# Layer scale on one Trainium2 core: the first four rows of y loaded as two partition halves on two DMA queues

## Chip, cores and metric

The kernel runs on one core of a Trainium2 chip. The time is device time in microseconds (us) of one execution, as a median of several; the profile is of one further execution, taken by the hardware profiler. A core has engines that run their own instruction streams: TensorE (PE, matrix products), VectorE (DVE, elementwise work), ScalarE (ACT), GpSimd (POOL) and SyncE (SP). Transfers between HBM and the on-chip memory (SBUF, 128 partitions) are issued by SP and ACT, each on a DMA queue (ring) of its own, and are carried out by 16 DMA engines that both queues share.

## The reference

```python
B, S, D = 1024, 16, 512
x, y:  normal * 0.05, shape (B, S, D), bfloat16
gamma: 1e-4 * normal * 0.05, shape (D,), bfloat16

def reference(x, y, gamma):
    return x + gamma * y
```

x, y and the output have 16,384 rows of 512 bfloat16 values, 16.78 MB each.

## The kernel before

The 16,384 rows are spread over 128 partitions, so that each partition has 128 rows. They are cut into blocks of 4, 64 and 60 rows per partition (`BLOCKS`, line 7); within a block, a partition's rows are contiguous in HBM, so a transfer of rows 4 to 68 moves one run of 64 KB for every partition, and a transfer of rows 0 to 4 one run of 4 KB. All of y stays in SBUF, in `y_sb`. x goes into the smaller `x_sb`, parts of which are used twice.

The order of everything is written out by hand. `SP` (line 12) and `ACT` (line 20) list what the two queues carry, in order: `('y', a, b)` loads rows a to b of y, `('x', a, b, at)` loads rows a to b of x to row `at` of `x_sb`, `('g',)` loads gamma's one row of 1 KB, `('s', a, b)` stores rows a to b of the result. Below, y(0,4) stands for the load of rows 0 to 4 of y, and so on. SP carries y(0,4), y(4,68), x(4,68), y(68,128), x(68,120), x(120,128). ACT carries x(0,4), gamma, and the stores of 4 to 68, 0 to 4 and 68 to 128.

`ring` (line 113) issues such a list. The first `EARLY` entries of a list are moved to the front of the program, ahead of the engines' opening synchronisation (line 197 on): two on SP, one on ACT. Ahead of entry number `AHEAD` (the same 2 and 1) the engine waits for its `s_held` semaphore. TensorE gives it out: it waits for the landing of `HOLD`, y(0,4) (line 147), and then frees SP, ACT and VectorE (line 148). So x(4,68) on SP and gamma on ACT are issued only after y(0,4) has landed, and a load into a part of `x_sb` that was used before waits for the adds that read it (`frees`, line 102): x(68,120) waits for the add of rows 24 to 68, x(120,128) also for the add of rows 0 to 8. The stores wait for `s_go`, which TensorE gives when `RELEASE`, x(68,120), has landed (line 157), and for the adds of their rows.

TensorE multiplies a row of ones with gamma (line 152), which puts gamma on all partitions of a PSUM tile, and VectorE copies that to `gamma_sb` (line 154). VectorE then works through `DVE` (line 28) on pieces of 8, 16, 44, 52 and 8 rows: `m` multiplies a piece of y by gamma in place (line 180), `a` adds x (line 189). The order is the multiplies of pieces 0, 1, 2, then the adds of pieces 2, 0, 1, then the multiplies of 3 and 4 and the adds of 3 and 4. Piece 0, rows 0 to 8, needs both y(0,4) and y(4,68). The last store, of rows 68 to 128, needs the adds of pieces 3 and 4.

A wait is `_take`, line 35: wait until the semaphore has a value, and take that off again.

Of the kernel before, what the change touches and what calls it, by code (L numbers as in the profile page):

```python
# [8 lines left out]
PIECES = [8, 16, 44, 52, 8]  # L9


SP = [
    ('y', 0, 4),
    ('y', 4, 68),
    ('x', 4, 68, 4),
    ('y', 68, 128),
    ('x', 68, 120, 24),
    ('x', 120, 128, 0),
]
ACT = [('x', 0, 4, 0), ('g',), ('s', 4, 68), ('s', 0, 4), ('s', 68, 128)]  # L20

EARLY = (2, 1)

HOLD, AHEAD = ('y', 0, 4), (2, 1)

RELEASE = ('x', 68, 120, 24)

# [4 lines left out]
def _take(sem, n, eng):  # L32


    return eng.wait_ge(sem, n).then_inc(sem, -n)  # L35


def kernel(
    tc: tile.TileContext,
    x: bass.AP,  # L40
    y: bass.AP,
    gamma: bass.AP,
    out: bass.AP,
):

    nc = tc.nc
    P = nc.NUM_PARTITIONS
    tc.close()  # L50
    tc.compile()  # L51

    xf = x.flatten_outer_dims()
    yf = y.flatten_outer_dims()
    of = out.flatten_outer_dims()
    N, D = xf.shape
    rows = N // P
    n = len(PIECES)
    assert sum(PIECES) == rows
    starts = [sum(PIECES[:c]) for c in range(n + 1)]  # L60
    dt = xf.dtype
    edges = [sum(BLOCKS[:c]) for c in range(len(BLOCKS) + 1)]
    assert edges[-1] == rows

    def rows_of(t, a, b):

        c = max(c for c in range(len(BLOCKS)) if edges[c] <= a)
        assert b <= edges[c + 1]
        block = t[P * edges[c] : P * edges[c + 1]].rearrange("(p n) d -> p n d", p=P)
        return block[:, a - edges[c] : b - edges[c], :]  # L70

    gamma_row = nc.alloc_sbuf_tensor("gamma_row", [1, D], dt).ap()
    ones_row = nc.alloc_sbuf_tensor("ones_row", [1, P], dt).ap()
    gamma_sb = nc.alloc_sbuf_tensor("gamma_sb", [P, D], dt).ap()
    y_sb = nc.alloc_sbuf_tensor("y_sb", [P, rows, D], dt).ap()
    x_loads = [w for w in ACT + SP if w[0] == "x"]
    y_loads = [w for w in SP + ACT if w[0] == "y"]
    stores = [w for w in SP + ACT if w[0] == "s"]
    for loads in (x_loads, y_loads, stores):
        assert sum(w[2] - w[1] for w in loads) == rows  # L80
    x_rows = max(w[3] + w[2] - w[1] for w in x_loads)
    x_sb = nc.alloc_sbuf_tensor("x_sb", [P, x_rows, D], dt).ap()
    gamma_ps = nc.alloc_psum_tensor("gamma_ps", [P, D], mybir.dt.float32).ap()

    sem = nc.alloc_semaphore
    s_gamma, s_ones, s_ps, s_dve = sem("s_gamma"), sem("s_ones"), sem("s_ps"), sem("s_dve")
    s_load = {w: sem("s_" + "_".join(map(str, w[:2]))) for w in x_loads + y_loads}
    s_held = {nc.sync: sem("s_held_sp"), nc.scalar: sem("s_held_act"), nc.vector: sem("s_held_dve")}
    s_add, s_go, s_rel, s_end, s_out = sem("s_add"), sem("s_go"), sem("s_rel"), sem("s_end"), sem("s_out")
    added = [a for kind, *a in DVE if kind == "a"]  # L90
    order = {a[0]: k for k, a in enumerate(added)}

    def meets(a, b, c, d):
        return a < d and c < b

    def pieces_of(a, b):
        return [c for c in range(n) if meets(starts[c], starts[c + 1], a, b)]

    def x_at(row):
        return next(w[3] + row - w[1] for w in x_loads if w[1] <= row < w[2])  # L100

    def frees(w):

        c = set()
        for v in x_loads[: x_loads.index(w)]:
            lo, hi = max(v[3], w[3]), min(v[3] + v[2] - v[1], w[3] + w[2] - w[1])
            if lo < hi:
                c |= set(pieces_of(v[1] + lo - v[3], v[1] + hi - v[3]))
        return sorted(c)

    early = []

    def ring(eng, what, n_early, n_ahead):

        known, went = 0, False
        for k, w in enumerate(what):
            kind = w[0]
            if k == n_ahead:
                _take(s_held[eng], 1, eng)
            need = frees(w) if kind == "x" else pieces_of(w[1], w[2]) + list(w[3:]) if kind == "s" else []  # L120
            need = max((order[c] + 1 for c in need), default=0)
            if kind == "s" and not went:
                _take(s_go, 1, eng)
                went = True
            if need > known:
                eng.wait_ge(s_add, need)
                known = need
            if kind == "g":
                i = eng.dma_start(out=gamma_row, in_=gamma.unsqueeze(0)).then_inc(s_gamma, 16)
            elif kind == "x":  # L130
                to = x_sb[:, w[3] : w[3] + w[2] - w[1], :]
                i = eng.dma_start(out=to, in_=rows_of(xf, w[1], w[2])).then_inc(s_load[w], 16)
            elif kind == "y":
                r = slice(w[1], w[2])
                i = eng.dma_start(out=y_sb[:, r, :], in_=rows_of(yf, w[1], w[2])).then_inc(s_load[w], 16)
            else:
                r = slice(w[1], w[2])
                i = eng.dma_start(out=rows_of(of, w[1], w[2]), in_=y_sb[:, r, :]).then_inc(s_out, 16)
            if k < n_early:
                early.append(i.ins)  # L140

    ring(nc.sync, SP, EARLY[0], AHEAD[0])
    ring(nc.scalar, ACT, EARLY[1], AHEAD[1])


    nc.vector.memset(ones_row, 1.0).then_inc(s_ones, 1)  # L146
    _take(s_load[HOLD], 16, nc.tensor)
    for s_one in s_held.values():
        nc.tensor.sem_inc(s_one, 1)
    _take(s_ones, 1, nc.tensor)  # L150
    _take(s_gamma, 16, nc.tensor)
    nc.tensor.matmul(gamma_ps, ones_row, gamma_row, start=True, stop=True).then_inc(s_ps, 1)  # L152
    _take(s_ps, 1, nc.vector)
    nc.vector.tensor_copy(out=gamma_sb, in_=gamma_ps).then_inc(s_dve, 1)  # L154
    _take(s_dve, 1, nc.vector)

    _take(s_load[RELEASE], 16, nc.tensor)
    nc.tensor.sem_inc(s_go, 1)
    nc.tensor.sem_inc(s_rel, 1)

    landed, open_mults = set(), 0

    def need(loads, c):
        for w in loads:
            if w not in landed and meets(starts[c], starts[c + 1], w[1], w[2]):
                if w == RELEASE:
                    _take(s_rel, 1, nc.vector)
                elif w == HOLD:
                    _take(s_held[nc.vector], 1, nc.vector)
                else:  # L170
                    _take(s_load[w], 16, nc.vector)
                landed.add(w)

    for kind, *args in DVE:
        c = args[0]
        yt = y_sb[:, starts[c] : starts[c + 1], :]
        if kind == "m":
            need(y_loads, c)
            g = gamma_sb[:, None, :].to_broadcast([P, PIECES[c], D])
            nc.vector.tensor_tensor(out=yt, in0=yt, in1=g, op=MULT).then_inc(s_dve, 1)  # L180
            open_mults += 1
        else:
            need(x_loads, c)
            if open_mults:
                _take(s_dve, open_mults, nc.vector)
                open_mults = 0
            at = x_at(starts[c])
            xt = x_sb[:, at : at + PIECES[c], :]
            nc.vector.tensor_tensor(out=yt, in0=xt, in1=yt, op=ADD).then_inc(s_add, 1)  # L189


    nc.scalar.sem_inc(s_end, 1)
    _take(s_end, 1, nc.sync)
    _take(s_add, n, nc.sync)
    _take(s_out, 16 * len(stores), nc.sync)

    main = nc.main_func.blocks[0].instructions
    names = {i.name for i in early}
    for b in nc.main_func.blocks[1:]:
        for i in [i for i in b.instructions if i.name in names]:  # L200
            b.instructions.remove(i)
    for k, i in enumerate(early):
        main.insert(1 + k, i)
# [30 lines left out]
```

## Time and profile before

| | |
|---|---|
| median of 3 runs | 119.87 us (119.71 to 120.06) |
| the profiled execution | 119.55 us |
| its span, first to last instruction | 118.2 us |
| multiplies, line 180 | 5 instructions, 34.7 us |
| adds, line 189 | 5 instructions, 34.7 us |
| DMA packets | 1442, 50.33 MB |
| landing after issue: y(0,4), 512 KB | 3.4 us |
| landing after issue: x(0,4), 512 KB | 4.2 us |
| landing after issue: last store, rows 68 to 128 | 23.8 us |

The span is cut into 40 slices in the page; the two rows below give the busy share of VectorE and of the 16 DMA engines in each (tenths).

```profile
DVE  0000200089999969999999999999999900000000
...
DMA  6999889988899879879969696898899889799793
```

A packet is counted whole in the slice in which it starts, so the DMA row swings. Lines of the profile that begin with an engine's name and a q (SPq, ACTq, DVEq) are that engine's sequencer: it issues transfers and waits. "Landing" is the arrival of the last of a transfer's completions.

### The profile page before, as it was taken

Reading aid. Unit: us, or ns where it says so; the run is one execution under the profiler, and the core shown is the slowest. Engines: PE = TensorE matmul, PEld = TensorE weight load, DVE = VectorE, ACT = ScalarE, POOL = GpSimd, SP = SyncE. Lnnn points to the kernel's source line nnn. Section 1 sums busy time; section 2 is a strip of 40 time slices with the busy share of each in tenths; the row PEclk is TensorE's granted clock in tenths of the full one; section 3 lists DMA queues with packets and bytes.
Section 4 is the critical chain, followed back from the end, with each engine's and each line's share of the span. In section 5 each row is a group of like instructions: output and inputs, shape, how many; then the busy total and the mean of one; then the engine's idle time right before and its main releaser. Section 6 shows DMA issues by size and latency. Waiting matters only on the chain. (4 is left out here: it accounts for less than half of the span.)

```text
span 118.2 us, 91 instructions
## 1 busy us (share of the span) xinstructions
PE 0.6 (0%) x1; PEld 0.1 (0%) x1; DVE 70.1 (59%) x12; POOL 0.2 (0%) x4
## 2 busy tenths in 40 slices
PE   0000100000000000000000000000000000000000
PEld 0000000000000000000000000000000000000000
DVE  0000200089999969999999999999999900000000
POOL 0000000000000000000000000000000000000000
DMA  6999889988899879879969696898899889799793
GB/s 248 461 666 399 355 355 399 665 355 355 355 599 466 355 333 624 374 333 499 499 288 576 288 576 288 360 637 355 355 576 488 355 355 510 333 582 416 333 499 166
DMA packets 1442, 50.33 MB, mean 426 GB/s; under 512 B 161, under 2 KB 162, under 8 KB 546
## 3 DMA queue, kind: packets, MB, share of 16 engines
q1 hardware_dynamic: 864, 33.03, 64.8%
q10 hardware_dynamic: 578, 17.30, 33.9%
HBM read 33.56 MB, written 16.78 MB: 426 GB/s over the span
## 5 line engine op out<-in xcount | busy, mean ns | idle before, releaser
L180 DVE TENSOR_TENSOR y_sb<-y_sb,gamma_sb 128x4096 bf16<-128x4096 bf16 (+3 forms) x5 | 34.7, 6981 | 10.9 <-DVEq L35 10.9
L189 DVE TENSOR_TENSOR y_sb<-x_sb,y_sb 128x4096 bf16<-128x4096 bf16 (+3 forms) x5 | 34.7, 6981 | 1.2 <-DVEq L35 1.1
L154 DVE CAST gamma_sb<-gamma_ps 128x512 bf16<-128x512 f32 x1 | 0.7, 692 | 10.2 <-DVEq L35 10.2
L146 DVE MEMSET ones_row<- 1x128 bf16 x1 | 0.2, 165 | 2.0 <-PEq L51 2.0
L152 PE MATMUL gamma_ps<-gamma_row,ones_row 1*128 1x512 bf16 x1 | 0.6, 581 | 11.6 <-PEq L35 11.6
L152 PEld LDWEIGHTS gamma_ps<-gamma_row,ones_row 1*128 1x128 bf16 x1 | 0.1, 101 | 11.6 <-issue 11.6
L218 POOL MEMSET const-bfloat16-1.0<- 128x1 bf16 x1 | 0.1, 101 | 0.0
L218 POOL MEMSET const-uint8-127<- 128x1 uint8 x1 | 0.1, 101 | 0.0
L218 POOL MEMSET const-float32-0.0<- 128x1 f32 x1 | 0.1, 98 | 0.2 <-issue 0.2
L218 POOL MEMSET const-float32-1.0<- 128x1 f32 x1 | 0.1, 98 | 0.0
## 6 DMA issues: line engine op xcount, KB each, us to landing
y_sb<-in_y_dram SPq DMA_DIRECT2D x1, 7680.0 KB, 57.3
out_dram<-y_sb ACTq DMA_DIRECT2D x1, 7680.0 KB, 23.8
x_sb<-in_x_dram SPq DMA_DIRECT2D x1, 6656.0 KB, 21.7
x_sb<-in_x_dram SPq DMA_DIRECT2D x1, 1024.0 KB, 22.0
y_sb<-in_y_dram SPq DMA_DIRECT2D x1, 512.0 KB, 3.4
x_sb<-in_x_dram ACTq DMA_DIRECT2D x1, 512.0 KB, 4.2
out_dram<-y_sb ACTq DMA_DIRECT2D x1, 512.0 KB, 22.3
y_sb<-in_y_dram SPq DMA_DIRECT2D x1, 23.4
```

Of the source, the lines that this page charges most:

```text
L146: nc.vector.memset(ones_row, 1.0).then_inc(s_ones, 1)
L152: nc.tensor.matmul(gamma_ps, ones_row, gamma_row, start=True, stop=True).then_inc(s_ps, 1)
L154: nc.vector.tensor_copy(out=gamma_sb, in_=gamma_ps).then_inc(s_dve, 1)
L180: nc.vector.tensor_tensor(out=yt, in0=yt, in1=g, op=MULT).then_inc(s_dve, 1)
L189: nc.vector.tensor_tensor(out=yt, in0=xt, in1=yt, op=ADD).then_inc(s_add, 1)
L218: nc = _bacc.Bacc("TRN2", target_bir_lowering=False, num_devices=1)
```

## The change

The load of rows 0 to 4 of y becomes two loads of 64 partitions each. The lower half is SP's first entry, the upper half is ACT's first entry, ahead of x(0,4). ACT now issues two entries early and two ahead of the hold. Both halves count up one semaphore, `s_hold`, and TensorE waits for 32 on it where it waited for 16. VectorE's wait for the hold is taken once, for the first half. The other edits carry the partition range of an entry through the helpers.

```diff
 SP = [
-    ('y', 0, 4),
+    ('y', 0, 4, 'half', 0),
     ('y', 4, 68),
...
-ACT = [('x', 0, 4, 0), ('g',), ('s', 4, 68), ('s', 0, 4), ('s', 68, 128)]
-
-EARLY = (2, 1)
-
-HOLD, AHEAD = ('y', 0, 4), (2, 1)
+ACT = [('y', 0, 4, 'half', 1), ('x', 0, 4, 0), ('g',), ('s', 4, 68), ('s', 0, 4), ('s', 68, 128)]
+
+EARLY = (2, 2)
+
+HOLD, AHEAD = [('y', 0, 4, 'half', h) for h in range(2)], (2, 2)
...
+    def parts_of(w):
+        return slice(P // 2 * w[-1], P // 2 * (w[-1] + 1)) if w[-2] == "half" else slice(0, P)
+
+    def at(sb, w, first):
+
+        return sb[parts_of(w), first : first + w[2] - w[1], :]
...
-    s_load = {w: sem("s_" + "_".join(map(str, w[:2]))) for w in x_loads + y_loads}
+    s_load = {w: sem("s_" + "_".join(map(str, w[:2] + w[4:]))) for w in x_loads + y_loads if w not in HOLD}
+    s_hold = sem("s_hold")
+    s_load |= {w: s_hold for w in HOLD}
...
-    _take(s_load[HOLD], 16, nc.tensor)
+    _take(s_hold, 16 * len(HOLD), nc.tensor)
...
-                elif w == HOLD:
-                    _take(s_held[nc.vector], 1, nc.vector)
+                elif w in HOLD:
+                    if w == HOLD[0]:
+                        _take(s_held[nc.vector], 1, nc.vector)
```

The instructions of TensorE, VectorE and GpSimd are the same and in the same order; SP's list has the same length, ACT's has one transfer more.

## The prediction

> **What bounds the kernel now.** I read the busy table and the 40 slices first, then the chain of waits, the timeline, and last narrow windows of the DMA columns.
>
> ```profile
> PE 0.6 (0%) x1; PEld 0.1 (0%) x1; DVE 70.1 (59%) x12; POOL 0.2 (0%) x4
> ...
> HBM read 33.56 MB, written 16.78 MB: 426 GB/s over the span
> ...
> issue 11%; DVE 3%
> ```
>
> VectorE, the busiest engine, has work for 59% of the span; the chain that ended last holds 14% of the span and is of no use here, because transfers ended it. 50.3 MB at 426 GB/s is the whole span: the kernel is one unbroken stream of transfers. It becomes longer only where the stream gets a hole. So the question is what each transfer that starts late waits for, and how much spare VectorE, which stands between loads and stores, has. The timeline gives the second:
>
> ```profile
> 0.00 0.85 SPq L135 DMA_DIRECT2D y_sb<-in_y_dram  x2
> 0.13 0.38 ACTq L132 DMA_DIRECT2D x_sb<-in_x_dram  x1
> ...
> 3.90 0.50 ACTq L129 DMA_DIRECT2D gamma_row<-in_gamma_dram  x1
> ...
> 11.59 0.58 PE L152 MATMUL gamma_ps<-gamma_row,ones_row 1*128 1x512 bf16 x1 [11.59 <-PEq L35]
> 12.32 0.69 DVE L154 CAST gamma_sb<-gamma_ps 128x512 bf16<-128x512 f32 x1 [10.16 <-DVEq L35]
> 23.95 18.43 DVE L180 TENSOR_TENSOR y_sb<-y_sb,gamma_sb 128x4096 bf16<-128x4096 bf16 x3 [10.94 <-DVEq L35]
> 43.45 18.43 DVE L189 TENSOR_TENSOR y_sb<-x_sb,y_sb 128x22528 bf16<-128x22528 bf16 x3 [1.08 <-DVEq L35]
> 55.37 2.53 SPq L132 DMA_DIRECT2D x_sb<-in_x_dram  x2
> 61.80 16.22 DVE L180 TENSOR_TENSOR y_sb<-y_sb,gamma_sb 128x26624 bf16<-128x26624 bf16 x2
> 77.41 17.36 ACTq L138 DMA_DIRECT2D out_dram<-y_sb  x3
> 78.17 16.23 DVE L189 TENSOR_TENSOR y_sb<-x_sb,y_sb 128x26624 bf16<-128x26624 bf16 x2
> ```
>
> Columns are start, duration, engine, line, operation. Gamma's 1 KB is issued at 3.90 but TensorE, whose only work needs it, starts at 11.59. It does no harm today: gamma_sb is ready at 12.32 + 0.69 = 13.01, and the first multiply waits for y until 23.95. After that VectorE has one hole of 1.08 us before 43.45 and then runs on until 94.4, when ACT issues the last store (77.41 + 17.36 - 0.34 = 94.43). Why gamma takes 7.7 us is in the windows (length, busy columns, clock, DMA share, GB/s; a packet counts whole where it starts, hence shares over 1):
>
> ```profile
> 0.00:1.00 1.00, 0.00 (x0) 0.00 (x0) 0.00 (x0) 0.20 (x4) 1.00 0.00 0
> 1.00:3.60 2.60, 0.00 (x0) 0.00 (x0) 0.17 (x1) 0.00 (x0) 1.00 0.98 384
> 3.60:4.00 0.40, 0.00 (x0) 0.00 (x0) 0.00 (x0) 0.00 (x0) 1.00 6.53 2744
> 4.00:6.00 2.00, 0.00 (x0) 0.00 (x0) 0.00 (x0) 0.00 (x0) 1.00 0.00 0
> 6.00:6.60 0.60, 0.00 (x0) 0.00 (x0) 0.00 (x0) 0.00 (x0) 1.00 4.05 1748
> 6.60:8.50 1.90, 0.00 (x0) 0.00 (x0) 0.00 (x0) 0.00 (x0) 1.00 0.00 0
> 8.50:9.00 0.50, 0.00 (x0) 0.00 (x0) 0.00 (x0) 0.00 (x0) 1.00 4.86 2099
> 9.00:10.90 1.90, 0.00 (x0) 0.00 (x0) 0.00 (x0) 0.00 (x0) 1.00 0.00 0
> 10.90:11.40 0.50, 0.00 (x0) 0.00 (x0) 0.00 (x0) 0.00 (x0) 1.00 4.85 2097
> ```
>
> From 1.0 to 3.6 the 16 engines run the 4 KB rows of y(0,4) and x(0,4), 1 MB in all. Then every engine starts a 64 KB row of y(4,68), and a new one every 2.42 us (3.7, 6.2, 8.6, 11.1). The packet records that these windows sum up have gamma's 1 KB at 8.63, after the second of them, and gamma's completion at 11.12, after the third. So beside a queue of 64 KB packets the other queue gets one packet in each 2.42 us, and a newcomer sits out the running packet and one more. x(0,4) escaped: all its eight packets per engine ran before the first 64 KB packet, though SP had issued y(4,68) by 0.85.
>
> [...] here 1.00 us (issue at 0.00, first bytes in the window from 1.00), and I use that.
>
> **The change part by part.** The sum is made on the profiled execution, 119.55 us (span 118.2 and 1.35 around it); the median of three is 119.87, 0.32 above.
>
> Bytes, VectorE's instructions and the order within each queue stay, but for one DMA more, ACT's half of y. The early issues cost nothing: ACT's second one (about 0.38 us more) lies ahead of the first bytes at 1.0, or beside the halves.
>
> The hold (TensorE waits for both halves, then frees SP, ACT and VectorE) falls from about 3.4 (landing of y(0,4)) to perhaps 2.8: half the bytes ahead of it, 8 x 0.16 = 1.3 us from 1.0, then about 0.4 to land. Worth nothing: what it frees on SP, x(4,68), stands behind y(4,68)'s 20 us of packets.
>
> What is moved is x(0,4): it was ACT's first transfer, and is now ACT's second, as y(4,68) is SP's second. SP issues y(4,68) at about 0.42, ACT can issue x(0,4) at 0.13 + 0.38 = 0.51. In the profile of before the queues' first packets come in the order of issue and over 1 us apart (SP 1.0, ACT 2.2, SP's second 3.65, by the packet records). So I take y(4,68) to reach the engines before x(0,4). Then x(0,4)'s eight packets an engine aren't run in a row (1.3 us) but one per 64 KB packet, and gamma stands behind them on ACT's queue.
>
> Count it on gamma's engine. First 64 KB packet at 1.0 + 8 x 0.16 = 2.3. x's first packet, a newcomer, runs after the second (as gamma did); its eighth and its completion after the eighth and ninth (SP's own completion of y(4,68) takes one turn at no cost), gamma after the tenth, gamma's completion after the eleventh. That is 11 x 2.42 + 8 x 0.16 = 27.9, so 30.2. In before, completion at 11.12 to gamma_sb at 13.01 is 1.9. The first multiply starts at 32.1 and not 23.95: 8.15 us late. The cover that hid gamma, y(4,68)'s landing (still near 23), is gone.
>
> Behind that wait stands all of VectorE. Of the 8.15 us, 1.08 go into the hole before 43.45. The rest, 7.07, moves the end of the add of rows 24 to 68 from 55.34 to 62.4, and SP's x(68,120), which waits for it, from 55.37 to 62.4, first bytes at 63.4. y(68,128) is through from 60.5 on, so the stream has a hole of up to 2.9 us, its first. ACT's last store moves from 94.43 to 101.5. In before its first packets ran at 99.29 (packet records) and with 1.0 us to the first byte 99.29 - 94.43 - 1.0 = 3.86 us were spare. End: 7.07 - 3.86 = 3.2 us later, which contains the earlier hole (both are limits on one stream). 119.55 + 3.2 = 122.75 profiled, and 119.87 + 3.2 = 123.1 as a median.
>
> Unknown: the pace at which queued DMAs are turned into packets. If it goes by DMA and not by rows, two short holes (halves of 0.6 us every 1.1 us, as 1.0 to 2.2 in before) open at the start: up to 1.0 us. Below nothing is excluded but for 0.1 us: the windows from 1.0 are already full at 0.98. I take nothing, and keep 1.0 as the upper end: this case's own range is 122.7 to 124.3.
>
> **The rivals.**
> One turn fewer (0.22): x's first packet runs after the first 64 KB packet. For it: the two issues are only 0.1 us apart. Against: gamma's two turns. 3.2 - 2.4 = 0.8: 120.7.
>
> More turns (0.18): the first 64 KB packet overtakes the last packets or the completion of ACT's half of y. For it: ACT's first packets came at 2.2 in before, later than SP alone would need for half of y. Against: x's completions in before all ran ahead of the 64 KB packets. One turn adds 2.4, two 4.8: 125.5 to 127.9; all five (four packets and the completion) give 135.
>
> No change (0.13), the other side: ACT's two early DMAs are both turned into packets before SP's second. Then x(0,4) runs whole before y(4,68), gamma lands near 11 as today, VectorE's spare of 1.08 + 3.86 = 4.94 us is not used up, and the stream is the same: 119.9. It decides by who is second at the engines; from gamma's completion at or before 27 (30.2 - 8.15 + 4.94) nothing is lost. For it: x(0,4) beat y(4,68) in before. Against: there x was ACT's first.
>
> Faster (0.04): the start gets shorter, y(4,68)'s long packets filling it sooner. The first 1.0 us is latency and stays, and 1.0 to 3.6 is at 384 GB/s against 426: at most 0.1 x 2.6 = 0.26 us, 119.6.
>
> **How the numbers follow.** Forecast 0.43, one turn fewer 0.22, more turns 0.18, no change 0.13, faster 0.04. A measurement of this kernel tells about 0.3% (0.36 us) from no change. Slower: 0.43 + 0.22 + 0.18 = 0.83; within 0.3%: 0.13 and, as 0.26 us is within it too, most of the 0.04, of which I leave 0.03 to faster for what I don't see; so 0.14 and 0.03. The range goes from the unchanged case, 119.8, to one turn more with part of the start's holes, 126.5, and leaves out the larger part of the case of more turns, and the gain.
>
> **What would show it.** Right: x(0,4) lands near 25 instead of 4.3; the matmul starts near 30.6 and the first multiply near 32; no idle before the adds of L189's first group but what VectorE itself makes; SP's x(68,120) issued near 62.4, with windows around 61 to 63 that start no packets; the last store issued near 101.5. Wrong: a matmul near 11 to 12 (x still goes ahead), or a first multiply at 26 to 29 (fewer turns), or a hold that comes after 5 (ACT's half of y is overtaken, more turns).

## The result and the profile after

The changed kernel takes 123.38 us (median of 4, 123.24 to 123.47) against 119.79 us before: ratio 1.0297, 95% interval 1.0274 to 1.0320, so 3.6 us slower. The forecast was 123.1. The profiled execution took 123.37 us, with a span of 122.0.

From the page of the changed kernel: the busy line, the HBM line, the chain's shares, and the two rows of slices.

```profile
PE 0.6 (0%) x1; PEld 0.1 (0%) x1; DVE 70.1 (57%) x12; POOL 0.2 (0%) x4
...
DVE  0000000000899999999999999999999991000000
...
HBM read 33.56 MB, written 16.78 MB: 412 GB/s over the span
...
issue 11%; DVE 2%
```

Bytes and VectorE's 70.1 us are unchanged. The rate over the span fell from 426 to 412 GB/s: the stream of transfers got holes, which the windows below show. VectorE's multiplies begin in the eleventh slice and not in the ninth.

From the timeline of the changed kernel (start, duration, engine, line, operation, idle before it):

```profile
0.00 1.18 SPq L144 DMA_DIRECT2D y_sb<-in_y_dram  x2
0.12 0.54 ACTq L144 DMA_DIRECT2D y_sb<-in_y_dram  x1
...
0.70 0.74 ACTq L142 DMA_DIRECT2D x_sb<-in_x_dram  x1
...
5.25 0.50 ACTq L140 DMA_DIRECT2D gamma_row<-in_gamma_dram  x1
...
29.96 0.58 PE L160 MATMUL gamma_ps<-gamma_row,ones_row 1*128 1x512 bf16 x1 [29.96 <-PEq L36]
...
31.76 18.43 DVE L189 TENSOR_TENSOR y_sb<-y_sb,gamma_sb 128x4096 bf16<-128x4096 bf16 x3 [0.37 <-DVEq L36]
50.33 18.43 DVE L198 TENSOR_TENSOR y_sb<-x_sb,y_sb 128x22528 bf16<-128x22528 bf16 x3
62.25 2.53 SPq L142 DMA_DIRECT2D x_sb<-in_x_dram  x2
...
81.21 20.43 ACTq L146 DMA_DIRECT2D out_dram<-y_sb  x3
```

TensorE gets gamma at 29.96 where it got it at 11.59, VectorE's first multiply starts at 31.76 where it started at 23.95, and from there VectorE runs without the 1.08 us hole ahead of the adds. x(68,120), which waits for the first add, is issued at 62.25 where it was issued at 55.37. x(0,4) itself lands at 25.5, long before the first add at 50.33, so nothing waits for it but gamma behind it.

Two stretches of windows of the changed kernel, the start and the region near 62 us (length, busy columns, clock, DMA share, GB/s; a packet counts whole where it starts):

```profile
0.00:1.30 1.30, 0.00 (x0) 0.00 (x0) 0.00 (x0) 0.20 (x4) 1.00 0.00 0
1.30:2.30 1.00, 0.00 (x0) 0.00 (x0) 0.00 (x0) 0.00 (x0) 1.00 0.89 213
2.30:3.35 1.05, 0.00 (x0) 0.00 (x0) 0.17 (x1) 0.00 (x0) 1.00 1.05 265
3.35:3.90 0.55, 0.00 (x0) 0.00 (x0) 0.00 (x0) 0.00 (x0) 1.00 5.33 1966
...
59.70:60.10 0.40, 0.00 (x0) 0.00 (x0) 0.40 (x1) 0.00 (x0) 1.00 5.68 2458
60.10:61.90 1.80, 0.00 (x0) 0.00 (x0) 1.80 (x1) 0.00 (x0) 1.00 0.00 0
61.90:63.20 1.30, 0.00 (x0) 0.00 (x0) 1.30 (x2) 0.00 (x0) 1.00 0.01 0
63.20:64.30 1.10, 0.00 (x0) 0.00 (x0) 1.10 (x1) 0.00 (x0) 1.00 2.36 775
```

The same place in the kernel before, where x(68,120) follows y(68,128) without a hole:

```profile
58.20:58.80 0.60, 0.00 (x0) 0.00 (x0) 0.60 (x1) 0.00 (x0) 1.00 3.78 1638
58.80:60.50 1.70, 0.00 (x0) 0.00 (x0) 1.70 (x1) 0.00 (x0) 1.00 0.00 0
60.50:61.10 0.60, 0.00 (x0) 0.00 (x0) 0.60 (x1) 0.00 (x0) 1.00 3.29 1420
```

Two things stand here. The start is slower: first bytes at 1.3 and not 1.0, and then 213 to 265 GB/s where the kernel before had 384, so that the 64 KB packets begin at 3.35 to 3.9 although half as many small packets run ahead of them. And near 62 there is a hole: the last packets of y(68,128), begun at 59.7 to 60.1, end near 62.1 (they take 2.27 us by the packet records), and the next start only from 63.2 on, spread over 1.1 us.

### The profile page after: what moved, and what is told of

It is laid out like the page before. It is cut to its first block, busy times and chain, and to the rows that moved or that the text cites. A ratio compares the mean times of both kernels' runs of the same rounds, so it can differ in the third digit from the quotient of the medians.

```text
span 122.0 us, 92 instructions
## 1 busy us (share of the span) xinstructions
PE 0.6 (0%) x1; PEld 0.1 (0%) x1; DVE 70.1 (57%) x12; POOL 0.2 (0%) x4
## 2 busy tenths in 40 slices
DMA packets 1458, 50.33 MB, mean 412 GB/s; under 512 B 177, under 2 KB 178, under 8 KB 562
## 6 DMA issues: line engine op xcount, KB each, us to landing
out_dram<-y_sb ACTq DMA_DIRECT2D x1, 7680.0 KB, 20.7
x_sb<-in_x_dram SPq DMA_DIRECT2D x1, 6656.0 KB, 18.6
x_sb<-in_x_dram ACTq DMA_DIRECT2D x1, 512.0 KB, 24.8
```

## The experiments

All times are medians; ratios are to runs of the kernel before (119.77 us) on the same chip. Except for e7 and e8, with one execution each, every kernel was run four times or more.

**e1: gamma and x(0,4) exchanged on ACT's queue.**

```diff
-ACT = [('y', 0, 4, 'half', 1), ('x', 0, 4, 0), ('g',), ('s', 4, 68), ...]
+ACT = [('y', 0, 4, 'half', 1), ('g',), ('x', 0, 4, 0), ('s', 4, 68), ...]
```

> The changed kernel with gamma and x(0,4) exchanged on ACT's queue, so gamma is early and x(0,4) waits for the hold. Theory (gamma behind x(0,4) makes VectorE late, and that opens the hole at x(68,120)): gamma's matmul near 9 to 12, first multiply at 24 to 25.5 when y(4,68) has landed, no hole near 62; only the slower start stays, which moved y(68,128)'s end by 1.3 us: 119.8 + 1.3 = 121.1. Rival (the two halves and their slow start cost all of it, gamma is hidden): 123.4 as before. Rival (gamma alone, the start is absorbed later): 119.8.

Measured: 120.97 us, ratio 1.0100 (1.0087 to 1.0113). From its timeline:

```profile
9.57 0.58 PE L160 MATMUL gamma_ps<-gamma_row,ones_row 1*128 1x512 bf16 x1 [9.57 <-PEq L36]
...
25.30 18.43 DVE L189 TENSOR_TENSOR y_sb<-y_sb,gamma_sb 128x4096 bf16<-128x4096 bf16 x3 [14.31 <-DVEq L36]
...
57.00 2.53 SPq L142 DMA_DIRECT2D x_sb<-in_x_dram  x2
```

The halves are still there, on both queues, and still slow at the start (first 64 KB packets at 3.6 to 4.0 by the packet records); only the places of gamma and x(0,4) differ, and 2.4 of the 3.6 us are gone. The multiply waits for y again (cast at 10.30, multiply at 25.30), and x(68,120) is issued at 57.00, ahead of the end of y(68,128). So gamma's place behind x(0,4) costs 2.4 us of the change, and 1.2 us are the slow start: what comes after is the same stream, that much later. e4 and e6 take the two away in the other order.

**e2: y whole, x(0,4) issued after the opening synchronisation** (the kernel before with one number changed).

```diff
-EARLY = (2, 1)
+EARLY = (2, 0)
```

> The kernel before, y(0,4) whole, with only one thing changed: x(0,4) is issued after the opening synchronisation (near 1.9 and not 0.13), so that it reaches the engines after y(4,68). Theory (queue order of x(0,4) and gamma): first 64 KB packets near 2.3, x(0,4) lands near 24 to 26, matmul near 28 to 31, first multiply at 30 to 32.5, x(68,120) issued at 60 to 62.8 against a stream that is through at 60.8: between 120.5 and 123.5. Rival (halves and their start are the cause): x(0,4) whole or late, 119.8.

Measured: 124.45 us, ratio 1.0392 (1.0378 to 1.0405), outside what either theory said and above the changed kernel. From its timeline:

```profile
1.90 0.39 ACTq L132 DMA_DIRECT2D x_sb<-in_x_dram  x1
...
31.08 0.58 PE L152 MATMUL gamma_ps<-gamma_row,ones_row 1*128 1x512 bf16 x1 [31.08 <-PEq L35]
...
63.36 2.53 SPq L132 DMA_DIRECT2D x_sb<-in_x_dram  x2
```

Nothing is halved here, and x(0,4) alone, 1.8 us later, costs 4.7 us. That shows the mechanism without the halves: x(0,4) comes after y(4,68) and lands 24.8 us after its issue, as in the changed kernel, where the packet records have its eight packets on an engine 2.58 us apart, one ahead of each 64 KB packet (6.3 to 24.3), and gamma stands behind them. It is worse than the change because x(0,4) sits out two 64 KB packets (they start at 2.49 and 5.08 by the packet records, x(0,4)'s first at 7.5), while in the changed kernel it sat out one. The difference that the record offers is when it came: here it is issued at 1.90, 0.6 us before the first 64 KB packet, so with 1.0 us from issue to first bytes, as at the start of the kernel before, it comes by this estimate while that runs; there it was issued at 0.70, 2.7 us before. The miss of 1 us is the end: x(68,120) was issued 0.6 us after the latest that I had expected, and a stream that starts again from nothing needs longer than I had allowed (below).

**e3: both halves of y on SP, x(0,4) first on ACT.**

```diff
 SP = [
     ('y', 0, 4, 'half', 0),
+    ('y', 0, 4, 'half', 1),
...
-ACT = [('y', 0, 4, 'half', 1), ('x', 0, 4, 0), ('g',), ('s', 4, 68), ...]
-EARLY = (2, 2)
+ACT = [('x', 0, 4, 0), ('g',), ('s', 4, 68), ...]
+EARLY = (3, 1)
```

`AHEAD` becomes (3, 1) as well.

> Both halves of y on SP, one after the other, x(0,4) first on ACT as before the change. Theory: x(0,4) reaches the engines before y(4,68) again, so gamma's matmul comes near 11 to 14 and the first multiply waits for y alone; what is left is the price of two 64-partition transfers at the start, whose packets took 0.28 us and not 0.16: 0.3 to 1.3 us, so 120.1 to 121.1. Rival (halves on any queue cost 3.6): 123.4.

Measured: 121.11 us, ratio 1.0123 (1.0097 to 1.0148), at the upper end of the theory's span. The matmul starts at 13.18, the first multiply at 25.48, after waiting 10.9 us for y. The halves alone, with gamma in time, cost 1.3 us, the same as in e1 within the intervals: the slow start belongs to the halves and not to the second queue.

**e4: split by rows, not by partitions.**

```diff
-    ('y', 0, 4, 'half', 0),
+    ('y', 0, 2),
...
-ACT = [('y', 0, 4, 'half', 1), ('x', 0, 4, 0), ('g',), ('s', 4, 68), ...]
+ACT = [('y', 2, 4), ('x', 0, 4, 0), ('g',), ('s', 4, 68), ...]
```

`HOLD` names the two new entries.

> The change with y(0,4) split by rows and not by partitions: rows 0 to 2 on SP, rows 2 to 4 on ACT, each on all 128 partitions in runs of 2 KB; the rest as in the changed kernel. Theory for the slow start (a 64-partition transfer runs at half rate): the first 64 KB packets start near 2.4 to 2.8 and not 3.4 to 3.9, gamma is late all the same (matmul near 28.5 to 31), end 122.3 to 123.4. Rival for the start (the number of rows that are turned into packets counts): 128 rows per part make it no earlier or later, first 64 KB packets at 3.4 or after, 123.4 or more.

Measured: 122.13 us, ratio 1.0204 (1.0188 to 1.0220), 0.2 us under the expected span, a miss: better than the theory said. The two windows of its start that matter:

```profile
1.00:2.60 1.60, 0.00 (x0) 0.00 (x0) 0.17 (x1) 0.00 (x0) 1.00 0.93 280
2.60:3.20 0.60, 0.00 (x0) 0.00 (x0) 0.00 (x0) 0.00 (x0) 1.00 4.55 1874
```

The 64 KB packets start at 2.6 and not 3.35: on all 128 partitions the same bytes, in twice as many packets, are through earlier, so the number of rows isn't what makes the halves slow. That a half runs at half the rate no run had shown by then; e7 measures it (205 GB/s beside 433). Gamma is late all the same (matmul at 28.76).

**e5: VectorE's order turned, so that x_sb comes free sooner** (the changed kernel otherwise).

```diff
-DVE = [('m', 0), ('m', 1), ('m', 2), ('a', 2), ('a', 0), ('a', 1), ...]
+DVE = [('m', 2), ('m', 0), ('a', 2), ('m', 1), ('a', 0), ('a', 1), ...]
```

> The changed kernel with VectorE's order turned so that the add that frees x_sb comes sooner: multiplies of pieces 2 and 0, add of 2, multiply of 1, then as before. VectorE's sum and its start near 31.8 stay, the last store is issued near 101.3 again, but x(68,120) is issued at 57.9 and not 62.25, ahead of the end of y(68,128). Theory (two limits close together: the hole at x(68,120), and behind it the last store, which then finds its queue empty): no hole near 62, one near 101 to 102, end 122.3 to 123.8. Rival (the hole at x(68,120) is all): the slow start alone is left, 121.1.

Measured: 122.37 us, ratio 1.0215 (1.0199 to 1.0230). Windows near 62 and near the last store:

```profile
62.00:62.40 0.40, 0.00 (x0) 0.00 (x0) 0.25 (x2) 0.00 (x0) 1.00 4.94 2130
99.50:101.10 1.60, 0.00 (x0) 0.00 (x0) 1.60 (x1) 0.00 (x0) 1.00 0.81 328
101.10:102.30 1.20, 0.00 (x0) 0.00 (x0) 0.41 (x1) 0.00 (x0) 1.00 0.00 0
102.30:102.80 0.50, 0.00 (x0) 0.00 (x0) 0.00 (x0) 0.00 (x0) 1.00 4.61 1966
```

The hole near 62 is closed: x(68,120)'s packets follow at once. A new one opens before the last store, which was issued at 101.54 (101.30 in the changed kernel). So a late VectorE meets two limits one behind the other; taking the first away gives 1.0 us, and the second holds the other 1.4 (e1, without both, is at 120.97). The rival, one limit alone, would have given 121.1.

**e6: split by rows, and gamma ahead of x(0,4)**: e4's and e1's edits together.

> Split by rows on both queues and gamma ahead of x(0,4) on ACT's: both costs of the change taken away, the two queues and the two transfers kept. Theory: matmul near 8 to 10, first multiply near 24.5, stream through with y(68,128) some 0.6 us later than in the kernel before (61.6 in the run split by rows, 61.0 before): 120.0 to 120.6. Rival (a second early transfer on ACT costs by itself): 121 or more.

Measured: 120.25 us, ratio 1.0044 (1.0028 to 1.0061). Two queues and an extra early transfer on ACT stay, and 3.1 of the 3.6 us are gone; no run takes the last 0.5 apart. It doesn't beat the kernel before: gamma at 4.3 is of no use to a multiply that waits for y until 24.27.

**e7 and e8: what a transfer on part of the partitions costs, on 8 MB.** In the kernel before, y(4,68) is cut into two transfers (e7) or three (e8), one behind the other on SP; `part` gives the partitions, and `EARLY` and `AHEAD` count the added entries.

```diff
-    ('y', 4, 68),
+    ('y', 4, 68, 'part', 0, 64),
+    ('y', 4, 68, 'part', 64, 128),
```

```diff
-    ('y', 4, 68),
+    ('y', 4, 68, 'part', 0, 32),
+    ('y', 4, 68, 'part', 32, 96),
+    ('y', 4, 68, 'part', 96, 128),
```

The 4.8 us for a slow packet in both expectations is an estimate, about twice the 2.42 us of the kernel before. Which ranges of partitions would be slow, and that 32 to 96 would not be, no run had shown before these two.

> A measurement, on the kernel before: y(4,68) as two 64-partition transfers (lower, upper) one behind the other on SP, 8 MB in all; y(0,4) whole, x(0,4) ahead on ACT. Theory (a 64-partition half [...] runs at half the rate): 64 KB packets take about 4.8 us and not 2.42, y(4,68) takes 38 us and not 19, end 119.8 + 19 = 139. Rival (halves cost only their issue): packets 2.42, 119.8 to 120.5.

> The same with y(4,68) as partitions 0 to 32, 32 to 96 and 96 to 128. Theory [...]: the middle's packets take 2.42 us, the outer ones' 4.8, end 119.8 + 9.6 = 129.4. Rival (any transfer on fewer than 128 partitions is slow by their number): middle as slow as a half, outer 32s slower still, 139 to 149. Rival (no cost): 119.8 to 120.5.

Measured, one execution each: 141.18 and 130.84 us, 2.2 and 1.4 above what was expected, because the slow packets take 5.12 us and not 4.8: 8 x (5.12 - 2.42) = 21.6 and 4 x (5.12 - 2.42) = 10.8, measured 21.4 and 11.1 over 119.77. Windows of e7, while the lower half is loaded:

```profile
3.90:4.30 0.40, 0.00 (x0) 0.00 (x0) 0.00 (x0) 0.00 (x0) 1.00 10.75 2478
4.30:8.40 4.10, 0.00 (x0) 0.00 (x0) 0.00 (x0) 0.00 (x0) 1.00 0.07 16
8.40:9.10 0.70, 0.00 (x0) 0.00 (x0) 0.00 (x0) 0.00 (x0) 1.00 6.86 1404
```

and of e8, at the end of partitions 0 to 32 and in the middle 64:

```profile
8.30:9.30 1.00, 0.00 (x0) 0.00 (x0) 0.00 (x0) 0.00 (x0) 1.00 5.12 1049
...
13.40:14.40 1.00, 0.00 (x0) 0.00 (x0) 0.00 (x0) 0.00 (x0) 1.00 2.93 1050
...
16.50:17.00 0.50, 0.00 (x0) 0.00 (x0) 0.00 (x0) 0.00 (x0) 1.00 4.84 2097
17.00:18.90 1.90, 0.00 (x0) 0.00 (x0) 0.00 (x0) 0.00 (x0) 1.00 0.00 0
18.90:19.40 0.50, 0.00 (x0) 0.00 (x0) 0.00 (x0) 0.00 (x0) 1.00 4.84 2097
```

Each burst is a new 64 KB packet on each engine. In a lower or upper half, and in the outer 32s, the bursts are some 5 us apart (5.12 us a packet by the records); in the middle 64 partitions 2.4 us, as on all 128. Sixteen packets of 64 KB in 5.12 us are 205 GB/s, in 2.42 us 433 GB/s. So in these runs it isn't the number of partitions that counts but which: both rivals of e8 fail. Why the ranges differ stands in no trace; what is shown is the rate of each.

## Why the prediction was right, and where its terms were off

**Gamma's wait.** Right, and shown by e1 (taken away alone, 2.4 us go) and e2 (made alone, without halves, 4.7 us). Matmul 29.96 against near 30.6, first multiply 31.76 against 32.1, x(0,4) landing at 0.70 + 24.8 = 25.5 against near 25, x(68,120) issued at 62.25 against 62.4, last store at 101.30 against 101.5.

**Two terms behind that were wrong and mostly cancelled.** The step "First 64 KB packet at 1.0 + 8 x 0.16 = 2.3" failed: it was 3.35 to 3.9. I had allowed up to 1.0 us for a pace of DMAs and taken nothing. The gap it was to stand for has its part: ACT's first packets ran at 2.33 by the packet records, 1.0 us after SP's at 1.34, so the halves ran nearly one after the other; what keeps them apart, no trace shows. But e4 has that gap too (1.00 and 1.98) and starts its 64 KB packets at 2.6. So I put most of the delay down to two things: the halves' 4 KB packets took 0.27 us in the mean (packet records), where those of y(0,4) and x(0,4) before took 0.17, and 64 KB packets on such halves ran at 205 GB/s in e7, beside 433 on all 128 partitions; and two of SP's issues took 1.18 us and not 0.85, with first bytes 0.3 us later. What two halves that run at the same time would reach, no run shows. And "x's first packet, a newcomer, runs after the second" failed: it ran after the first, at 6.3 to 6.5 by the packet records, which is one turn, 2.4 us, less. Gamma had been a newcomer beside 64 KB packets (issued at 3.90, they began at 3.65); x(0,4) was issued well before them (0.70 against 3.38). e2, where it came after them, shows the two turns. The rival "one turn fewer" was thus right about the turn; with the late start the sum came near my forecast and not near its 120.7. That the number was met to 0.3 us is in this part luck: an error of one turn too many and one of a start more than 1 us too early.

**The end.** "3.86 us were spare" before the last store, hence 3.2 us, put the limit in the wrong place. In the changed kernel the stream was late already and the last store's queue never empty: issued at 101.30, it stood behind the store of rows 0 to 4, whose packets began at 101.50 to 103.39 (packet records). What sets the end is x(68,120): its landing frees the stores. The page's landing times, added to the issue, show it:

```
kernel        x(68,120) issued + to landing = landed   span    span - landed
before        55.37 + 21.7 = 77.1                      118.2   41.1
after         62.25 + 18.6 = 80.9                      122.0   41.1
e1            57.00 + 21.7 = 78.7                      119.8   41.1
e2            63.36 + 18.8 = 82.2                      123.4   41.2
e3            56.88 + 21.7 = 78.6                      119.7   41.1
e4            61.04 + 18.6 = 79.6                      120.8   41.2
e5            57.91 + 20.7 = 78.6                      121.1   42.5
e6            55.83 + 21.7 = 77.5                      118.7   41.2
```

The end is the landing of x(68,120) plus 41.1 us (41.1 in e7 and e8 as well), with e5 as the exception that has the second hole. An estimate says why it is a constant: what is still to move then, x(120,128) and the stores, is 17.83 MB, and 17.83 MB in 41.1 us is 434 GB/s, the rate of full 64 KB packets (433). By that estimate the stretch has no slack, and a late last store costs nothing (issued at 94.43 before and at 101.30 after, 41.1 both times) until it opens a hole there, as in e5 (42.5). Behind packets still queued x(68,120) landed 21.7 us after its issue (before, e1, e3, e6; 20.7 in e5); from nothing it is 18.6 (after, e4; 18.8 in e2), where eight packets of 1.966 us (packet records) make 15.7. My 1.0 us to the first byte was right (63.2 after 62.25) but short: the engines start over 1.1 us and their first packets take 2.0 to 3.1 us. The hole itself was shorter than my "up to 2.9 us", because the slow start had moved y(68,128)'s end from 60.8 to 62.1. The two again made up for each other.

**The halves and the second queue.** The forecast took no gain and no loss for the halves themselves, an assumption that no run had shown: they lose 1.2 us (e1) or 1.3 us (e3). In the change this comes on top of what gamma's place costs: with rows in place of halves, e4, everything behind the start is 1.2 us earlier (matmul 28.76 against 29.96, x(68,120) issued 61.04 against 62.25), and the end too. Four kernels, us:

```
            gamma behind x(0,4)   gamma ahead of x(0,4)
halves      123.38 (change)       120.97 (e1)
rows        122.13 (e4)           120.25 (e6)
```

So gamma's place costs 2.4 us beside the halves and 1.9 beside the rows, and the halves cost 1.2 or 0.7 more than the rows, by which of the two is taken away first.

**The hold.** I had it fall to 2.8; it rose. ACT's half landed at 0.12 + 4.6 = 4.7, y(0,4) before at 3.4. ACT's half wasn't overtaken, its last completion ran at 3.88 by the packet records. As said there, nothing hangs on the hold: x(4,68) stood behind y(4,68) anyway, its packets ran from 24.48 on (packet records).

Left open: why the first packets after a hole are slow. The runs show it for loads (18.6 us from issue to landing in the changed kernel and e4, 18.8 in e2, where eight packets make 15.7); e5's last store, issued into an empty queue at 101.54, landed after 19.5 us, of which eight packets of 2.27 us (packet records) are 18.2, so a store lost only 1.3 us where loads lost 2.9. No run was made to tell why.

## What to carry to other kernels

In these runs a short transfer isn't parallel to a long one that is queued on the other queue: on each engine it gets one packet per long packet (2.58 us apart in the changed kernel: x(0,4) landed 24.8 us after its issue, and 4.2 where it ran first), and what stands behind it, here gamma's 1 KB, waits for all its turns (its packet ran at 26.91, and at 8.63 before). So before moving a transfer, ask which of two queues' second entries is now first at the engines, and what 1 KB stands at the end of the shorter one. Put the tiny operand that an engine's whole work needs ahead of bulk that is needed later, and split a load by rows rather than at partition 64 (0.7 to 1.2 us here).

## What the runs showed of the hardware that was not expected

A 64-partition load ran at 205 GB/s on partitions 0 to 64 and 64 to 128 (e7) but at 433 GB/s on 32 to 96 (e8). A transfer on the other queue sat out one 64 KB packet where it was issued 2.7 us before the first of them (x(0,4) in the changed kernel, first packet at 6.3), and two where it came while they ran (x(0,4) in e2, 7.5; gamma in the kernel before, 8.63); that the time of arrival decides it is inferred from these. A load stream that ran dry lost, from issue to landing, 18.6 - 15.7 = 2.9 us.
